# Banded attention beside a gated MLP on one NeuronCore: 64-key blocks, and two head groups on the two partition halves

## The chip, the cores and the metric

The kernel runs on one core of a Trainium2 chip. Its metric is the device time of one execution, in microseconds (us). Three runs of the kernel before took 259.98, 260.29 and 259.19 us; their median is 259.98 us. The core has five engines that run side by side and wait for each other through semaphores: TensorE (PE: matmuls, each preceded by a weight load, PEld), VectorE (DVE), ScalarE (ACT), GpSimd (POOL) and SyncE (SP, which here issues DMAs). Matmul results go to PSUM, which has eight banks of 512 float32 columns on each of 128 partitions.

## The reference

```python
xn = layernorm(x)                                   # x: 2048 tokens x 512
# A: attention, 32 heads of 16, a band of 256 keys back from each query
q, k, v = split(xn @ wqkv)
scores  = q @ k.T * 16 ** -0.5
mask    = (i - j >= 0) & (i - j < 256)
o       = softmax(where(mask, scores, -1e9)) @ v
# B: gated MLP with a 2048 x 2048 mix over tokens
z       = gelu(xn @ w_in); z1, z2 = z[..., :688], layernorm(z[..., 688:])
g       = w_sp @ z2 + b_sp[:, None]
out     = x + o @ wo + (z1 * g) @ w_out             # bfloat16 in and out
```

## The kernel before

The first stage (to about 84 us of the span) normalizes and transposes x, computes z (`zp`, L280), and most of the 48 units of q, k and v (`pj_`, L111 and L129). q is stored twice with the odd or the even heads zeroed (`qpad`), so that a strip of 32 partitions holds two heads, e = 0 and 1, and a *group* G of 8 heads fills 128 partitions as four strips s. v is stored with a column of ones behind each head, so that P times V also gives the softmax's sums.

The second stage is written out by hand: the string `ORDER` is a list of steps, and the program issues them in that order on every engine.

- `S` takes the next block of scores (`do_scores`). For a pair of query tiles J (256 queries) and a group G there are two kinds, "P" and "Q": four strips of a 32-row by 128-column tile of the array (128 keys, the columns are queries of two heads), 8 matmuls of 256 columns. A third kind, "D", serves two groups at once: the corners of the band, in 32 x 64 tiles, 32 matmuls of 128 columns. Each `S` fills two tiles of the PSUM pool `ps_s` (three tiles of two banks), and ACT takes the exponential of each tile into `E` or `ED` (L608, L583).
- `m` multiplies the result by a 0/1 mask on DVE (L611).
- `p` is P times V of one (J, G) (`pv`, L519): 56 matmuls in 128 x 32 tiles, four at a time, for the four strips. Their output `o` is one bank of the pool `ps_x` (two banks). DVE transposes it (L526). For the corners a copy `vh` of v with one half of the partitions zeroed is loaded by DMA (`load_half`).
- `n` divides by the sums and transposes again (`normalize`, L532 to L542) into `oT`.
- `q`, `g`, `f` begin a unit of the last four v tiles, of the token mix (`gf`, L433, 16 matmuls of 344 columns) or of the output (`fo`, L469 and L476, 10 matmuls of 512 columns: six with `uT`, four with `oT`); a number goes on with the unit for so many matmuls. These use the whole 128 x 128 array and the pool `ps_x`. After the last `g` of a tile, u is transposed by a DMA into `uT`, and `f` adds x and stores.

So PE's order is fixed: runs of whole-array matmuls, with `S` and `p` set between them. `check_sums` looks at all softmax sums at the end (after output tile 13); a branch recomputes attention with the maximum subtracted if a sum is out of range.

Of the kernel before, what the change touches and what calls it, by code (L numbers as in the profile page):

```python
# [8 lines left out]
P = 128  # L9
# [5 lines left out]
S_TOK = 2048  # L15
# [3 lines left out]
VW = DH + 1  # L19
VROW = H * VW + DH  # L20
F = 1376
# [13 lines left out]
PAD = 64  # L35
NM = NB + 1
# [4 lines left out]

ORDER = """
S q4 q4 S q4 q4 S g m 8 S m 8 g3 S 7 S m 6 p S p S g n m 8 S m 8 g3 S n 7 S m 6 g2 S 11 S 3
g m 6 S m 10 S p p S g n m 11 S n 5 g5 S m 11 S p p S f n m 7 S 3 g m 5 S n 11 S p p S g n m
10 S m 6 f3 S m 7 S p p S g n n 10 S m 6 g4 S m n 12 f1 S m 6 S 3 g5 S m 11 S p p S f n m 7
S 3 g m 5 S n 11 S p p S g n m 10 S 6 g m 4 S m 12 S p p S f n n 6 S 4 f m 3 S m 7 g1 S m 9
S n 6 g4 S m 12 S p p S f n m 6 S 4 g m 5 S n 11 S p p S f n m 7 S 3 g m 5 S m 11 S p p S g
n n 16 S f m m 6 S 4 g n 4 S m 12 S p p S g n m 9 S m 7 f2 S n 7 S 1 f m 10 S p p S g n m 16
g1 S m n 8 S 7 g m 16 S p p S g n n 16 g1 S m 15 f1 S m 6 S 3 g5 S m 11 S p p S g n m 16 f1
S m 9 S p g n m 16 g n 16 p f n 10 f10 f10 f10  # L50
"""

@with_exitstack
def kernel(
# [22 lines left out]
    kT = pers.tile([P, NG, PAD + S_TOK], BF, name="kT")  # L77
    v_y = pers.tile([P, NM, VROW], BF, name="v_y")
# [4 lines left out]
    maskY = pers.tile([P, P], BF, name="maskY")  # L83
    maskD = pers.tile([P, P], BF, name="maskD")
    maskC = pers.tile([P, PAD], BF, name="maskC")
# [5 lines left out]
    xnT = pq.tile([P, NC, PAD + S_TOK], BF, name="xnT")  # L91
    wqkv = pq.tile([P, NC, 3 * D], BF, name="wqkv")
    r_all = pers.tile([P, NJ * NG, 16], F32, name="r_all")
# [10 lines left out]
    def qkv_unit(b, i, k):  # L104
        t0 = PAD + b * 512
# [20 lines left out]
        else:  # L126
# [7 lines left out]
            parts = [(0, PAD, NB), (PAD, P, 0)] if m == 0 else [(0, P, m)]  # L134
            for p0, p1, mo in parts:
                nc.vector.tensor_copy(
                    out=v_y[p0:p1, mo, 0 : H * VW].rearrange("p (h w) -> p h w", w=VW)[:, :, 0:DH],
                    in_=pt[p0:p1, :].rearrange("p (h d) -> p h d", d=DH),
                )

    qkv_list = [(b, i) for b in range(4) for i in range(12) if (b, i) != (0, 8)] + [(0, 8)]

    with ExitStack() as actx:
# [54 lines left out]
        def setup_late():  # L198
            nc.vector.memset(kT[:, :, 0:PAD], 0.0)
# [5 lines left out]
            nc.vector.memset(v_y[0:PAD, 0, :], 0.0)  # L205
            nc.vector.memset(v_y[PAD:P, NB, :], 0.0)
            nc.vector.tensor_tensor(
                out=maskC[:], in0=maskD[:, 0:PAD], in1=maskD[:, PAD:P], op=ALU.add
            )

        for m, off in ((maskY, 0), (maskD, -PAD)):
            nc.gpsimd.memset(m[:], 1.0)
            nc.gpsimd.affine_select(
                out=m[:, 0:PAD], in_=m[:, 0:PAD], pattern=[[-1, PAD]],
                compare_op=ALU.is_gt, fill=0.0, base=off, channel_multiplier=1,
            )
            nc.gpsimd.affine_select(
                out=m[:, PAD:P], in_=m[:, PAD:P], pattern=[[1, PAD]],
                compare_op=ALU.is_ge, fill=0.0, base=PAD + off, channel_multiplier=-1,
# [42 lines left out]
        def transposes(n, xn):  # L262
            if n >= 8:
                nc.sync.dma_start_transpose(
                    out=xnT[:, :, PAD + n * P : PAD + (n + 1) * P], in_=xn[:]
# [7 lines left out]
            nc.scalar.copy(out=xnT[:, :, PAD + n * P : PAD + (n + 1) * P], in_=tp[:])  # L273

        def z_half(n, half):
            zp = ps_s.tile([P, 2, 512], F32, name="zp", tag="S")
            for c in range(NC):
                for j in range(2):
# [3 lines left out]
                        lhsT=xnT[:, c, PAD + n * P : PAD + (n + 1) * P],  # L282
# [43 lines left out]
        for n in range(NB):  # L326
# [7 lines left out]
            if n == NB - 3:  # L334
                nc.vector.tensor_copy(out=xnT[:, :, 0:PAD], in_=xnT[:, :, S_TOK : PAD + S_TOK])
# [46 lines left out]
    ep = ctx.enter_context(tc.tile_pool(name="ep", bufs=4))  # L382
    cp = ctx.enter_context(tc.tile_pool(name="cp", bufs=2))

    late_ctx = ctx.enter_context(ExitStack())
    late_pool = []
    v_half = []

    def late():
        if not late_pool:  # L390
# [5 lines left out]
            for i in range(2):  # L396
                vh = late_pool[0].tile([P, 4, VROW], BF, name=f"vh{i}")
                nc.gpsimd.memset(vh[PAD:P, 0:2, :], 0.0)
                nc.gpsimd.memset(vh[0:PAD, 2:4, :], 0.0)
                v_half.append(vh)  # L400
        return late_pool[0]

    def load_half(J):
        late()
        vh = v_half[J % 2]
        nc.sync.dma_start(out=vh[0:PAD, 0:2, :], in_=v_y[0:PAD, 2 * J + 1 : 2 * J + 3, :])
        if J > 0:
            nc.sync.dma_start(out=vh[PAD:P, 2:4, :], in_=v_y[PAD:P, 2 * J - 2 : 2 * J, :])
# [53 lines left out]
    def f_work(t, c0):  # L462
# [11 lines left out]
        q0 = (1 - t % 2) * P  # L474
# [15 lines left out]
    ED = {}  # L490
# [3 lines left out]
    def pv(J, G):  # L494
        Et = E[(J, G)]
        Ed = ED[(J, G // 2)]
        g = G % 2
        o = ps_x.tile([P, 512], F32, name="o", tag="f")
        for e in range(2):
            c0 = e * 256  # L500
            vh = v_half[J % 2]
# [50 lines left out]
    def do_scores(J, G, kind):  # L552
# [12 lines left out]
        if kind == "D":  # L565
            ED[(J, G // 2)] = late().tile([P, 32, PAD], BF, name="ED", bufs=2)
            if G == 0 and J == 0:
                load_half(0)
# [295 lines left out]
```

## Time and profile before

| | |
|---|---|
| median of 3 runs | 259.98 us (259.19 to 260.29) |
| profiled execution | 259.87 us, span 258.2 us |
| PE busy | 252.7 us, 98% of the span, 3877 matmuls |
| ACT busy | 196.5 us, 76% |
| DVE busy | 205.1 us, 79% |
| second stage: first `S` to last output add | 84.1 to 255.1 us |
| ACT in 100 to 200 us of the span | 18.96 to 19.75 us busy in each 20 us |
| chain that ended last | PE 96% |
| granted TensorE clock | 1.00 |

A busy PE here means that some matmul was in flight. Matmuls overlap, so the time that a block of them takes is read from the start of its first to the start of what follows it.

### The profile page before, as it was taken

The numbers are of one execution on the slowest core, as the hardware profiler recorded it, in microseconds if no ns is written. First come the engines' busy times: TensorE is split into PE (matmuls) and PEld (weight loads), VectorE is DVE, ScalarE is ACT, GpSimd is POOL, SyncE is SP. The second block draws the span as 40 slices with busy tenths as digits, with TensorE's granted clock in tenths as the row PEclk, the third lists the DMA queues.
The fourth block names the chain that finished last, engine by engine and source line by source line (L and its number), as shares of the span: only waits on it lengthen the run. The fifth ranks groups of instructions, "written<-read, shape, count | busy, mean of one in ns | idle before, by whom it ended". The sixth has DMA issues, their size and how long they took to land.

```text
span 258.2 us, 8833 instructions
## 1 busy us (share of the span) xinstructions
PE 252.7 (98%) x3877; PEld 142.4 (55%) x3877; DVE 205.1 (79%) x425; ACT 196.5 (76%) x236; POOL 20.2 (8%) x49
## 2 busy tenths in 40 slices
PE   8999999999999999999999999999999999999994
PEld 2665555555555455655654655555564655646553
DVE  4895997875657889598889689898889978858784
ACT  2777547456456899999999999999998988689600
POOL 4120312111011240000000000000000000000000
PEclk9999999999999999999999999999999999999999
DMA  7994021027400207575244709654637644654332
GB/s 218 369 252 143 0 43 41 0 45 124 79 0 4 62 6 156 112 158 94 68 66 135 173 28 159 106 138 82 98 43 177 84 116 90 120 111 108 74 55 67
DMA packets 64683, 25.85 MB, mean 100 GB/s; under 512 B 53649, under 2 KB 63169, under 8 KB 64641
## 3 DMA queue, kind: packets, MB, share of 16 engines
q1 hardware_dynamic: 63152, 24.22, 44.4%
q10 hardware_dynamic: 1488, 1.03, 1.3%
q8 instruction: 31, 0.51, 0.8%
q14 instruction: 12, 0.09, 0.1%
HBM read 8.41 MB, written 2.10 MB: 41 GB/s over the span
## 4 chain that ended last, share of the span: by engine, by line
PE 96%; DVE 1%; DMA 1%; issue 0%; POOL 0%
PE gf L433 31%; PE zp L280 15%; PE S L558 11%; PE o L519 9%; PE fo L469 9%; PE pj_o L111 7%; PE fo L476 6%; PE pj_f L111 4%; PE pj_f L129 3%; PE pj_o L129 2%; DMA xt<-in_A_x_dram 1%; PE tp L270 1%; DVE stats L228 1%; POOL rs L238 0%; DVE xo L481 0%
## 5 line engine op out<-in xcount | busy, mean ns | idle before, releaser
L608 ACT ACTIVATE E<-S 128x1024 bf16<-128x1024 f32 (+1 forms) x128 | 117.6, 1007 | 8.7 <-PE S L558 8.5
L433 PE MATMUL gf<-z2n,wspT 128*128 128x344 bf16 x512 | 83.3, 310 | 0.0
L433 PEld LDWEIGHTS <-wspT 128*128 128x128 bf16 x512 | 46.7, 98 | 28.6 <-issue 5.5
L280 PE MATMUL zp<-w_in_sb,xnT 128*128 128x344 bf16 x256 | 41.7, 309 | 0.0
L611 DVE TENSOR_TENSOR E<-E,maskY 128x2048 bf16<-128x2048 bf16 (+2 forms) x36 | 37.9, 1058 | 2.5 <-ACT E L608 2.4
L280 PEld LDWEIGHTS <-xnT 128*128 128x128 bf16 x256 | 24.8, 98 | 15.3 <-ACT xnT L273 0.2
L558 PE MATMUL S<-qpad,kT 32*64 32x128 bf16 (+1 forms) x1008 | 32.9, 246 | 0.1
L583 ACT ACTIVATE ED<-S 128x1024 bf16<-128x1024 f32 x32 | 31.0, 1023 | 2.3 <-PE S L558 2.3
L526 DVE STREAM_TRANSPOSE ot<-o 128x512 f32<-128x512 f32 x32 | 22.3, 715 | 8.4 <-PE o L519 8.3
L558 PEld LDWEIGHTS <-kT 32*64 32x64 bf16 (+1 forms) x1008 | 12.3, 98 | 22.7 <-issue 21.6
L469 PE MATMUL fo<-w_out_sb,uT 128*128 128x512 bf16 (+1 forms) x102 | 24.6, 368 | 0.0
L439 DVE SCALAR_TENSOR_TENSOR u<-gf,b_all,z 128x344 bf16<-128x344 f32 x32 | 18.2, 567 | 7.3 <-PE gf L433 6.4
L519 PE MATMUL o<-E,v_y 128*32 128x128 bf16 (+1 forms) x736 | 23.3, 239 | 0.3 <-issue 0.3
L519 PE MATMUL o<-ED,vh 128*32 128x64 bf16 x960 | 21.2, 193 | 0.0
L111 PE MATMUL pj_o<-xnT,wqkv 128*128 128x512 bf16 x80 | 20.5, 379 | 0.0
L287 ACT ACTIVATE z<-zp 128x688 bf16<-128x688 f32 x16 | 11.9, 743 | 11.1 <-PE zp L280 11.1
L287 ACT ACTIVATE z2n<-zp 128x688 bf16<-128x688 f32 x16 | 11.9, 743 | 10.3 <-PE zp L280 10.3
L111 PEld LDWEIGHTS <-wqkv 128*128 128x128 bf16 x128 | 12.5, 98 | 12.6
L122 DVE TENSOR_SCALAR qpad<-qt,hmask 128x512 bf16<-128x512 bf16 x32 | 9.7, 346 | 12.2 <-ACT qt L120 12.2
L611 DVE TENSOR_TENSOR ED<-ED,maskC 128x2048 bf16<-128x2048 bf16 x16 | 19.4, 1210 | 0.0
L476 PE MATMUL fo<-wo_sb,oT 128*128 128x512 bf16 (+1 forms) x68 | 17.7, 368 | 0.0
L519 PEld LDWEIGHTS <-v_y 128*32 128x32 bf16 x736 | 15.2, 97 | 4.0 <-issue 3.6
(68 smaller groups left out, 234.8 us busy)
## 6 DMA issues: line engine op xcount, KB each, us to landing
vh<-v_y SPq DMA_DIRECT2D x15, 140.0 KB, 3.5
xo<-in_A_x_dram SPq DMA_DIRECT2D x16, 128.0 KB, 3.4
out_dram<-xo SPq DMA_DIRECT2D x15, 128.0 KB, 2.0
xt<-in_A_x_dram SPq DMA_DIRECT2D x3, 512.0 KB, 9.8
wqkv<-in_A_wqkv_dram SPq DMA_DIRECT2D x1, 1536.0 KB, 10.2
w_in_sb<-in_B_w_in_dram ACTq DMA_DIRECT2D x2, 344.0 KB, 5.8
w_in_sb<-in_B_w_in_dram SPq DMA_DIRECT2D x2, 344.0 KB, 5.4
w_out_sb<-in_B_w_out_dram SPq DMA_DIRECT2D x1, 640.0 KB, 6.1
```

The lines of the kernel that those rows point to most:

```text
L111: nc.tensor.matmul(pt[:], lhsT=wqkv[:, c, w0 : w0 + P], rhs=xnT[:, c, t0 : t0 + 512], start=(c == 0), stop=(c == NC - 1),)
L280: nc.tensor.matmul(zp[:, j, 0:HALF], lhsT=xnT[:, c, PAD + n * P : PAD + (n + 1) * P], rhs=w_in_sb[:, c, f0 : f0 + HALF], start=(c == 0), s ...
L287: nc.scalar.activation(out=dst.rearrange("p (j f) -> p j f", j=2), in_=zp[:, :, 0:HALF], func=ACT.Gelu_apprx_tanh,)
L433: nc.tensor.matmul(gf[:, 0:HALF], lhsT=wspT[t][:, c, :], rhs=z2n[:, c, j * HALF : (j + 1) * HALF], start=(c == 0), stop=(c == NB - 1),)
L469: nc.tensor.matmul(fo[:, 0:w], lhsT=uTs[t][:, ch, :], rhs=w_out_sb[:, ch, c0 : c0 + w], start=(ch == 0), stop=False,)
L476: nc.tensor.matmul(fo[:, 0:w], lhsT=oTs[t // 2][:, c, q0 : q0 + P], rhs=wo_sb[:, c, c0 : c0 + w], start=False, stop=(c == NC - 1),)
L519: nc.tensor.matmul(o[32 * s : 32 * s + 32, c0 + r0 : c0 + r0 + n], lhsT=v[:, m, h * VW : h * VW + 32], rhs=rhs(s), start=(i == 0), stop=(i ...
L526: nc.vector.transpose(out=ot[:].rearrange("p b j -> p (b j)"), in_=o[:])
L558: nc.tensor.matmul(out, lhsT=kT[32 * s : 32 * s + 32, g, k0 : k0 + nk], rhs=qpad[J // 2][32 * s : 32 * s + 32, g, :, qs - q00 : qs - q00 + ...
L583: nc.scalar.activation(out=Ed[:, 16 * i : 16 * i + 16, :], in_=S[i][:].rearrange("p b (x q) -> p (b x) q", q=PAD), func=ACT.Exp, scale=SM_ ...
L608: nc.scalar.activation(out=o, in_=w, func=ACT.Exp, scale=SM_SCALE)
L611: nc.vector.tensor_tensor(out=out, in0=in0, in1=mask.unsqueeze(1).to_broadcast([P, in0.shape[1], in0.shape[2]]), op=ALU.mult,)
```

## The change

Keys are cut into blocks of 64 where they were cut into tiles of 128. A pair of query tiles then sees eight key blocks, and each block serves a run of 64-query pieces (one to four). The table `BURSTS` lists these as (block, first piece, pieces, column), packed into five `S` steps of 256 columns each (three for J = 0), with no separate corner kind. All scores use 32 x 64 tiles: two head groups at once, one on each half of the output partitions. So `E` holds 64 keys of one group on partitions 0 to 63 and 64 keys of the other on 64 to 127. P times V contracts over 64 rows and handles both groups at once in 64 x 32 tiles, eight at a time: 128 matmuls for each J and pair of groups (64 for J = 0), with an output of two banks that now comes from `ps_s`, the pool of the scores. Where a group's v lies on the other half of the partitions, it is loaded across by DMA (`load_cross`) in place of `load_half`. The masks shrink to 1024, 2048 and 1024 columns for each J and pair of groups. `E` has one buffer for each pair of groups where it had four in all. The 64-token shift of the keys (`PAD`) goes, and `ORDER` is a new list: 76 `S` (80 before), 16 `p` (32), 48 `m` (48), the same `q`, `g` and `f`.

```diff
-PAD = 64
+KB = 64
+EW = 5 * 256
+BURSTS_FIRST = [
+    [(4, 0, 4, 0)],
+    [(7, 3, 1, 256), (5, 1, 3, 320)],
+    [(6, 2, 2, 512)],
+]
+BURSTS = [
+    [(3, 0, 4, 0)],
+    [(4, 0, 4, 256)],
+    [(2, 0, 3, 512), (7, 3, 1, 704)],
+    [(0, 0, 1, 768), (5, 1, 3, 832)],
+    [(1, 0, 2, 1024), (6, 2, 2, 1152)],
+]
+MASKS_FIRST = [(0, 64), (256, 128), (512, 64)]
+MASKS = [(192, 128), (640, 256), (1088, 128)]
 ORDER = """
-S q4 q4 S q4 q4 S g m 8 S m 8 g3 S 7 S m 6 p S p S g n m 8 S m 8 g3 S n 7 S m 6 g2 S 11 S 3
...
-S m 9 S p g n m 16 g n 16 p f n 10 f10 f10 f10
+S q4 q4 S q4 m q3 S 1 g6 S 10 S g3 m 2 m 4 m S 5 m 1 p m S 1 g9 p n S 7 g1 S 3 n 4 m 4 S 4 f1 m
+3 S 6 S g9 m p S 7 g1 S 1 m 10 S 4 g6 S 9 m 1 S g6 m 3 S 6 n 1 f1 p S 6 S 3 n g7 S 9 S f7 S 3 g3
+m 1 m S 11 S 1 f1 m 5 S m 4 g1 p S 5 m 3 S 3 m 4 g5 S 4 m 4 S 3 g5 p S 4 n 5 S 2 g9 S 1 n 6 f2 S
+6 S 1 m 1 g2 m 1 m 3 S 6 m 2 p S 1 m 1 g6 S 4 n 4 p S 2 g8 S 8 g1 S m 7 m 2 m S 6 f3 S 1 n 6 S
+f2 m 3 p S 3 m 2 g1 S 2 m 10 S 3 g9 S p 6 S 1 f5 S 5 g4 n S 4 n 5 S 3 g9 S 4 m 3 f1 S 7 m 1 S 1
+g3 m 4 S 8 p S 1 g4 m 4 S m 8 g2 S 4 m 6 S 4 f4 p S 6 S g5 n 5 S 4 m 2 g1 m 3 S 10 n 1 S m 1 g9
+m S 7 f1 m p S 4 m 3 S 2 f3 p S 3 m 4 S g9 S 1 m 6 g4 S 6 m 2 n 1 p S 3 g7 S 2 n 3 m 4 g1 n 1 S
+7 m 2 S 5 f8 m 2 f1 p 7 n 2 f10 f10 f10
 """
...
+    def load_cross(J):
+        vx = cp.tile([P, 2, VXROW], BF, name="vx", bufs=3)
+        v_cross[J] = vx
+        nc.gpsimd.memset(vx[:, :, 3 * VG :], 0.0)
+        for h in range(2):
+            own, other = slice(h * KB, h * KB + KB), slice(KB - h * KB, P - h * KB)
+            nc.sync.dma_start(
+                out=vx[own, :, 0 : 3 * VG],
+                in_=v_y[other, 2 * J : 2 * J + 2, h * VG : (h + 3) * VG],
+            )
...
+    def pv(J, g):
+        Et = E.pop((J, g))
+        o = ps_s.tile([P, 2, 512], F32, name="S", tag="S")
+        terms = sorted((t for burst in bursts(J) for t in burst), key=lambda t: -t[2])
+        n = len(terms)
+        terms = [terms[i // 2 if i % 2 == 0 else n - 1 - i // 2] for i in range(n)]
         for e in range(2):
+            for i, (k, i0, ni, c0) in enumerate(terms):
+                m = 4 * J - 4 + k
                 for s in range(4):
+                    for h in range(2):
+                        part = slice(h * KB, h * KB + KB)
...
+                        q0 = e * 256 + i0 * KB
+                        nc.tensor.matmul(
+                            o[32 * s : 32 * s + 32, h, q0 : q0 + ni * KB],
+                            lhsT=v, rhs=Et[part, s, e, c0 : c0 + ni * KB],
+                            start=(i == 0), stop=(i == n - 1),
+                        )
+        ot = late().tile([P, 2, 16, 32], F32, name="ot", bufs=2)
+        turned[(J, g)] = ot
+        nc.vector.transpose(
+            out=ot[:].rearrange("p h b j -> p (h b j)"), in_=o[:].rearrange("p h c -> p (h c)")
+        )
...
+    def do_scores(J, g, burst):
+        if burst == 0:
+            pool = late() if (2 * J + g) % 2 else ep
+            E[(J, g)] = pool.tile([P, 4, 2, EW], BF, name=f"E{g}")
+            if g == 1 and J + 1 < NJ:
+                load_cross(J + 1)
+        S = [ps_s.tile([P, 2, 512], F32, name="S", tag="S") for _ in range(2)]
+        terms = bursts(J)[burst]
+        b0 = min(t[3] for t in terms)
+        for k, i0, ni, c0 in terms:
+            k0 = (4 * J - 4 + k) * KB
+            q0 = J % 2 * 256 + i0 * KB
+            for s in range(4):
+                for h in range(2):
+                    o = S[s // 2][h * KB : h * KB + KB, s % 2, :]
+                    nc.tensor.matmul(
+                        o.rearrange("p (e q) -> p e q", e=2)[:, :, c0 - b0 : c0 - b0 + ni * KB],
+                        lhsT=kT[32 * s : 32 * s + 32, 2 * g + h, k0 : k0 + KB],
+                        rhs=qpad[J // 2][32 * s : 32 * s + 32, 2 * g + h, :, q0 : q0 + ni * KB],
+                        start=True, stop=True,
+                    )
+        w = sum(t[2] for t in terms) * KB
+        Et = E[(J, g)]
+        for i in range(2):
+            nc.scalar.activation(
+                out=Et[:, 2 * i : 2 * i + 2, :, b0 : b0 + w].rearrange("p s e q -> p (s e) q"),
+                in_=S[i][:].rearrange("p s (e q) -> p (s e) q", e=2)[:, :, 0:w],
+                func=ACT.Exp, scale=SM_SCALE,
+            )
```

`normalize` does for two groups at once what it did for one (one reciprocal of 32 sums, two multiplications, one transpose of 512 columns), and `do_mask` multiplies the three column ranges of `MASKS` with one mask tile for both halves.

More of the change, by code (lines that the diff above doesn't have):

```diff
@@ L529, in normalize, with bursts @@
[L529 to L540 removed]
+    def bursts(J):
+        return BURSTS if J else BURSTS_FIRST
@@ L793 @@
     rows = []
-    masks = [x for x in groups if x[2] != "P"]
-    units = [(J, G) for J in range(NJ) for G in range(NG)]
+    masks = [(J, g, i) for J, g in pairs for i in range(3)]
+    units = list(pairs)
+    load_cross(0)
     work = {
```

280 lines of the change are left out of this document (87 added, 193 removed).

## The prediction

> **What bounds the kernel now.** First the page's busy table, its slices and its chain:
>
> ```profile
> PE 252.7 (98%) x3877; PEld 142.4 (55%) x3877; DVE 205.1 (79%) x425; ACT 196.5 (76%) x236; POOL 20.2 (8%) x49
> ...
> ACT  2777547456456899999999999999998988689600
> ...
> PE 96%; DVE 1%; DMA 1%; issue 0%; POOL 0%
> ```
>
> PE sets the end, and in the stage of `ORDER` (84 to 255 us) ACT is full as well. So a gain must come out of PE's time, and ACT must not become later. Next, ACT's groups with their shapes kept apart:
>
> ```profile
> L608 ACT ACTIVATE E<-S 128x1024 bf16<-128x1024 f32 x120 | 113.7, 1033 | 8.7 <-PE S L558 8.5
> L583 ACT ACTIVATE ED<-S 128x1024 bf16<-128x1024 f32 x32 | 31.0, 1023 | 2.3 <-PE S L558 2.3
> L608 ACT ACTIVATE E<-S 128x512 bf16<-128x512 f32 x8 | 4.4, 623 | 0.0
> ```
>
> An exponential of 1024 columns costs 113.7 / 120 = 0.95 us, a step `S` 1.9 us. Third, PE's timeline around one `p p`, to see what a block of small tiles costs (start, length, ..., the lengths overlap, so differences of starts count):
>
> ```profile
> 132.02 0.40 PE L558 MATMUL S<-qpad,kT 32*128 32x256 bf16 x8
> 132.34 0.35 PE L519 MATMUL o<-E,v_y 128*32 128x256 bf16 x8
> 132.52 0.23 PE L519 MATMUL o<-ED,vh 128*32 128x64 bf16 x8
> 132.58 0.23 PE L519 MATMUL o<-E,v_y 128*32 128x128 bf16 x4
> 132.63 0.23 PE L519 MATMUL o<-ED,vh 128*32 128x64 bf16 x8
> 132.69 0.34 PE L519 MATMUL o<-E,v_y 128*32 128x256 bf16 x8
> 132.86 0.23 PE L519 MATMUL o<-ED,vh 128*32 128x64 bf16 x8
> ...
> 133.81 0.43 PE L558 MATMUL S<-qpad,kT 32*64 32x128 bf16 x32
> 134.17 1.63 PE L433 MATMUL gf<-z2n,wspT 128*128 128x344 bf16 x10
> 135.73 0.52 PE L558 MATMUL S<-qpad,kT 32*128 32x256 bf16 x8
> ```
>
> Four tiles at once: two rounds of 64 columns take 0.057, a round of 128 takes 0.057, 256 and 128 together 0.166, so 256 alone 0.11. The D block (32 matmuls, eight tiles at once) takes 0.36. Ten `gf` of 0.146 take 1.56, so leaving a run of whole-array matmuls costs 0.10; every change of tile shape does. The trace's starts within a round lie 3.3 ns apart, weight loads between them.
>
> Last, a place where PE stands still in the middle of a `p`:
>
> ```profile
> 125.11 0.22 PE L519 MATMUL o<-E,v_y 128*32 128x128 bf16 x1
> 125.65 0.24 PE L519 MATMUL o<-E,v_y 128*32 128x128 bf16 x3 [0.32 <-issue]
> ```
>
> No buffer or operand ends this wait. Against a round of 0.057 it costs 0.49. The page's DMA table explains it:
>
> ```profile
> q8 instruction: 31, 0.51, 0.8%
> ```
>
> These 31 packets and 0.51 MB for PE's 2 x 3877 instructions are PE's code, some 250 instructions (125 matmuls) each. Two of three such stops lie at PE's records 2496 and 4288, 7 x 256 apart, the third at 3008: boundaries of 256 instructions. In the DMA records a packet starts 0 to 3.1 us after PE passes a boundary (once 1.0 before), takes 1.0 to 1.4, and at those three stops PE went on 1.4 to 1.5 after the packet's end. So the next 256 instructions must not be used up sooner than 3 to 4 us. In the rest of the stage they last 3.5 to 10 us, but for one span.
>
> **The change, part by part,** against the profiled execution's own 259.87 us (span 258.2 and 1.7 around it; the median is 259.98).
>
> *P times V.* The two G of a J took 1.46 (chain rows of x112) in 13 cases, 2 x 0.79 in the last, for J = 0 2 x 0.56 and 1.0: 19.0 + 1.6 + 2.1 = 22.7. After, a step has for each e rounds of 256, 64, 256, 64, 192, 128, 192 and 128 columns: 2 x (0.110 + 0.028 + 0.083 + 0.057) = 0.56, twice 1.11, with the shape change and the first loads 1.23; for J = 0 half the rounds, 0.67. 14 x 1.23 + 2 x 0.67 = 18.5: **-4.2**. It supposes that 64 x 32 tiles run eight at once, which no row shows; the nearest are D (eight at once, 32 x 64) and this `p` (four at once). Bounds: -4.2, and +12.5 (each round doubled). I take -4.2: D has both row strips and column halves.
>
> *Scores.* A single round of 512 columns in eight tiles costs what two rounds of 256 in four tiles do, 0.33; steps of two rounds 0.34 to 0.36. Five sum to 1.70, before 4 x 0.33 + 0.36 = 1.68: +0.02 x 14. J = 0 has three steps (0.91) for five (1.46), twice: -1.1. Sum **-0.85**.
>
> *The new order.* It cuts the whole-array work into 77 runs where there were 66: 11 x 0.10 = **+1.1**.
>
> *Waits for PSUM.* `p` now takes a tile of the pool of three. The next `S` then needs both exponentials of the one before it, and the second `S` after `p` the DVE transposition of o. Counted off `ORDER`, two `S` with a `p` between stand 2.5 to 3.1 us apart; needed are 0.12 + 0.30 (from the first matmul of an S to the last, from there to ACT) + 0.90 + 1.02 (two exponentials back to back) + 0.09 (to PE) = 2.4. The second `S` comes 1.6 us or more after `p`; needed are 0.3 + about 1.25 (512 columns take 0.72). So both waits are just covered, nothing taken; if DVE is in a mask of 1.2 us then, up to 0.5 each, 8 in all. Two waits of `S` for ACT before (J = 0, at 96.1 and 110.0, the blocks 0.61 and 0.57 long for 0.36 and 0.33) have no counterpart: **-0.45**.
>
> *ACT* sheds 4 full and 4 half exponentials, 6 us of 149; 143 us fit into 84 to 240 us, `S` standing 2.05 apart on average for 1.9 of ACT. *DVE* loses a third of its mask columns (-19 us), joins two transpositions into one: hidden, PE is later. *DMA*: eight crossings of two DMAs for 15 of `vh`, on SP's queue in the same places, a J ahead, with tiny memsets on POOL in front of `u`'s, a tile ahead: nothing; if late, `p` waits up to the 3.5 us of a landing, once a J. `E`'s single buffer per pair is freed by a `p` that `ORDER` puts ahead of the next pair's first `S`: nothing.
>
> *The tail.* After the last `p`, DVE's chain to the output is longer: transposition 1.25 for 0.72, two multiplications, one transposition of 512: +1.25, then the add, `check_sums` (1.8) and the next add free PSUM for the last `fo`. It waited 0.1 to 0.2 before, now about 1.1: **+0.9**.
>
> Sum so far -3.5: 256.4.
>
> *Code.* Some 4053 matmuls for 3877, and a full `p` is 256 instructions, one whole packet, run in 1.23 us. Where a boundary falls shortly ahead of a `p`, the next 256 are gone in the `p` and an `S`. Laying the costs above along `ORDER` (two instructions a matmul), 12 of 26 boundaries of the stage have the next one 2.3 to 3.1 us later. Before, only three spans were as short: 3.16 and 3.03 (stops of 0.13 and 0.32) and 2.76, whose packet came early (no stop). From PE's passing to usable code, the 25 packets of that stage needed 1.5 to 5.7 us, mostly 2.9 to 3.9. Bounds for the 12: nothing, and (3.7 - 2.7) x 12 = 12, or 16 where transfers collide with packets. I take 0.55 each, **+6.6**, more than the two stops of like spans because the spans are shorter, less than the middle of all packets because a boundary ahead of a `p` is read early while PE still has whole-array work. The stops of before (0.49 + 0.32 + 0.13) go: **-0.9**. Sum -3.5 + 6.6 - 0.9 = +2.2: **262.1 us**.
>
> [...]
>
> **The rivals.**
> 1. *The code comes in time: faster.* If PE's sequencer stands 64 instructions ahead, as the packet that came 1.0 early suggests, it passes a boundary 1.5 us before PE does and the spans suffice. Stops under 3.5 in all: 255.5 to 259.0, most likely 256.5. [...] For it: 22 of 25 boundaries cost nothing. Against: the spans there were longer. It decides when a packet is usable 2.6 us after the boundary.
> 2. *Packets behind DMA transposes.* At 120.98 and 164.84 the packet came 2.3 and 3.1 us after PE, amid `wspT` transfers. At 0.85 to 1.2 us for each of the 12, 10 to 14 in all: 265.5 to 269.5, say 267.
> 3. *The row halves of P times V do not overlap.* A `p` costs 2.34, 1.23 twice: +12.5 on P times V in place of -4.2, so 255.5 + 16.7 = 272, with the code stops gone, since such a `p` gives a packet time. For it: no row has this tile. Against: D. [...]
>
> **How the numbers follow.** The forecast 0.50 (stops of 3.5 to 10: 259 to 265.5), rival 1 0.30, rival 2 0.13, rival 3 0.07. A measurement tells some 0.5% (1.3 us) from no change: faster is below 258.7, slower above 261.3. Rival 1 gives 0.28 faster and 0.02 same; of the forecast a third is within: 0.17; the rest, 0.53, is slower. The range from 255.5 to 268.5 leaves out rival 3 and the edges.
>
> **What would show it.** Right: waits "issue" on PE, on matmuls or loads inside or just after L524's `o`, some ten of 0.2 to 1.5 us, 128 matmuls apart or a multiple; an undisturbed `p` of 1.23; `S` of 0.33 to 0.36. Rival 1: no such waits, span near 255. Rival 2: waits over 1 us beside a full DMA slice. Rival 3: rounds of 256 columns 0.22 apart. The prediction is wrong in another way if PE waits for ACT at the `S` after a `p`, or for DVE at the one after that.

## The result, and the profile after

The changed kernel takes **270.81 us** (median of 4 runs, 269.12 to 273.33), the kernel before beside it 260.13: ratio **1.039, 95% interval 1.033 to 1.046** (the run of 273.33, 1.6% above the fastest, counts as slow and is left out of the ratio). The prediction was 262.1 in a range of 255.5 to 268.5, with a chance of 0.53 for slower. The sign is right, the time is outside the range. The profiled execution of after took 271.59 us with a span of 269.8: 11.6 more than the span of before. All accounts below are made on these two spans.

From the page of after, the busy table, PE's slices, the chain that ended last and the code packets:

```profile
PE 249.7 (93%) x4029; PEld 137.7 (51%) x4053; DVE 178.6 (66%) x367; ACT 192.0 (71%) x228; POOL 16.6 (6%) x52
...
PE   6999999999998999798999898999999989799980
...
q8 instruction: 32, 0.52, 0.9%
...
PE 86%; issue 4%; DVE 3%; DMA 2%; ACT 2%; SPq 1%; POOL 0%; DVEq 0%
```

PE was busy 98% of a shorter span before and 93% now, and "issue" stands in the chain with 4%, where it had 0. So the longer time is PE standing still, not PE working more. (24 of the 4053 matmul records are missing in this trace, all of matmuls of 512 columns; each leaves 0.22 without a start, and six waits of `fo` for "issue" in the trace, of 0.2 each, are no more than that.) L576 is the scores `S`, L442 is `gf`, L478 is `fo`. L524 is `p`: the view calls its output S as well, since it takes a tile of that pool. What PE waited for, in the view of waits (us in total, times, longest):

```profile
PE S L524 <- issue: 2.4, 2, 1.6
PE S L576 <- issue: 2.2, 3, 1.4
...
PE S L576 <- DVE r_all L539: 1.2, 1, 1.2
...
PE S L576 <- ACT E L585: 1.1, 2, 0.7
PE gf L442 <- issue: 1.1, 1, 1.1
...
PE fo L478 <- DVE xo L490: 0.9, 1, 0.9
```

"Issue" stops lie inside `p`, inside `S` and inside `gf`: no one kind of work, and no buffer. Two of them in PE's timeline (start, length, ..., the idle time before in brackets):

```profile
111.04 0.40 PE L576 MATMUL S<-qpad,kT 32*64 32x384 bf16 x9
112.86 0.26 PE L576 MATMUL S<-qpad,kT 32*64 32x128 bf16 x7 [1.42 <-issue]
...
235.37 0.24 PE L524 MATMUL S<-E,v_y 64*32 64x192 bf16 x1 [1.59 <-issue]
```

An `S` stops after 9 of its 16 matmuls. Counting PE's weight loads from the start, eight stops lie where 96 + 128 k pairs of load and matmul have gone, that is 256 instructions or a multiple apart (a q8 packet has 16384 bytes), at 112.86, 126.00, 151.47, 164.71, 168.44, 218.14, 235.37 and 246.97, and each ends 1.31 to 1.60 us after the end of a q8 packet. Taken between starts, less the usual distance, they cost 1.58, 0.80, 1.28, 0.56, 0.97, 1.26, 1.75 and 0.35 us: 8.55, where before had 0.94. The one at 218.14 is the row "DVE r_all" above, and the one at 164.71 is part of "ACT E": the view names the last operand that came, the records the packet that ended 1.31 and 1.34 before.

The rest came at the end. Records of the final branch in the two traces, which no view of busy time shows (start in us, length in ns; the rest of each line is put together from the records after it):

```
before  256.12   352  PE  COMPARE_BRANCH   next instruction: PE 0.41 us, DVE 0.60 us after its branch; span ends 2.04 after
after   264.69  4082  PE  COMPARE_BRANCH   next instruction: PE 4.14 us, DVE 3.43 us after its branch; span ends 5.12 after
```

A code packet of PE starts at 265.71 and ends at 267.48, while PE stands in that branch.

### The profile page after: what moved, and what is told of

Its sections match the earlier page's. It is cut to its first block, busy times and chain, and to the rows that moved or that the text cites. A ratio compares the mean times of both kernels' runs of the same rounds, so it can differ in the third digit from the quotient of the medians.

```text
span 269.8 us, 9076 instructions
## 1 busy us (share of the span) xinstructions
PE 249.7 (93%) x4029; PEld 137.7 (51%) x4053; DVE 178.6 (66%) x367; ACT 192.0 (71%) x228; POOL 16.6 (6%) x52
## 4 chain that ended last, share of the span: by engine, by line
PE 86%; issue 4%; DVE 3%; DMA 2%; ACT 2%; SPq 1%; POOL 0%; DVEq 0%
PE gf L442 29%; PE zp L291 14%; PE S L576 10%; PE S L524 8%; PE fo L478 6%; PE pj_o L128 5%; PE fo L485 5%; PE pj_f L128 4%; PE pj_o L146 3%; PE pj_f L146 2%; ACT E L585 1%; DMA xt<-in_A_x_dram 1%; DVE xo L490 1%; DMA vx<-v_y 1%; SPq L463 1%
## 5 line engine op out<-in xcount | busy, mean ns | idle before, releaser
L585 ACT ACTIVATE E<-S 128x1024 bf16<-128x1024 f32 x152 | 142.6, 1015 | 24.5 <-PE S L576 23.5
L442 PE MATMUL gf<-z2n,wspT 128*128 128x344 bf16 x512 | 85.7, 310 | 1.1 <-issue 1.1
L442 PEld LDWEIGHTS <-wspT 128*128 128x128 bf16 x512 | 45.7, 98 | 32.7 <-issue 12.3
L291 PE MATMUL zp<-w_in_sb,xnT 128*128 128x344 bf16 x256 | 41.9, 309 | 0.0
L604 DVE TENSOR_TENSOR E<-E,maskFD 128x1024 bf16<-128x1024 bf16 (+2 forms) x48 | 38.2, 812 | 5.1 <-ACT E L585 4.9
L576 PE MATMUL S<-qpad,kT 32*64 32x512 bf16 (+3 forms) x960 | 33.4, 310 | 4.7 <-issue 2.2
L531 DVE STREAM_TRANSPOSE ot<-S 128x1024 f32<-128x1024 f32 x16 | 20.0, 1250 | 22.8 <-PE S L524 22.8
L576 PEld LDWEIGHTS <-kT 32*64 32x64 bf16 x960 | 11.4, 102 | 27.0 <-issue 25.7
L478 PE MATMUL fo<-w_out_sb,uT 128*128 128x512 bf16 (+1 forms) x87 | 23.1, 365 | 2.3 <-issue 1.0
L524 PE MATMUL S<-E,v_y 64*32 64x256 bf16 (+2 forms) x960 | 21.9, 231 | 1.6 <-issue 1.6
L524 PE MATMUL S<-E,vx 64*32 64x256 bf16 (+2 forms) x960 | 21.9, 232 | 0.8 <-issue 0.8
L524 PEld LDWEIGHTS <-vx 64*32 64x32 bf16 x960 | 18.1, 90 | 6.5 <-issue 6.4
L490 DVE TENSOR_TENSOR xo<-fo,xo 128x512 bf16<-128x512 f32 (+1 forms) x17 | 11.1, 656 | 13.4 <-PE fo L485 13.3
L524 PEld LDWEIGHTS <-v_y 64*32 64x32 bf16 x960 | 18.9, 90 | 1.5 <-issue 1.5
L139 DVE TENSOR_SCALAR qpad<-qt,hmask 128x512 bf16<-128x512 bf16 x32 | 9.7, 345 | 11.3 <-ACT qt L137 11.3
```

The lines of the kernel that those rows point to most:

```text
L291: nc.tensor.matmul(zp[:, j, 0:HALF], lhsT=xnT[:, c, n * P : (n + 1) * P], rhs=w_in_sb[:, c, f0 : f0 + HALF], start=(c == 0), stop=(c == NC ...
L442: nc.tensor.matmul(gf[:, 0:HALF], lhsT=wspT[t][:, c, :], rhs=z2n[:, c, j * HALF : (j + 1) * HALF], start=(c == 0), stop=(c == NB - 1),)
L478: nc.tensor.matmul(fo[:, 0:w], lhsT=uTs[t][:, ch, :], rhs=w_out_sb[:, ch, c0 : c0 + w], start=(ch == 0), stop=False,)
L524: nc.tensor.matmul(o[32 * s : 32 * s + 32, h, q0 : q0 + ni * KB], lhsT=v, rhs=Et[part, s, e, c0 : c0 + ni * KB], start=(i == 0), stop=(i = ...
L531: nc.vector.transpose(out=ot[:].rearrange("p h b j -> p (h b j)"), in_=o[:].rearrange("p h c -> p (h c)"))
L576: nc.tensor.matmul(o.rearrange("p (e q) -> p e q", e=2)[:, :, c0 - b0 : c0 - b0 + ni * KB], lhsT=kT[32 * s : 32 * s + 32, 2 * g + h, k0 : ...
```

## Two theories

*Code:* PE, and at the branch DVE too, wait for their next instructions; what counts is where the boundaries of 256 instructions fall in the work, and where the target of the final jump (over the body of the branch, which these inputs don't run) lies. *Tiles:* the time lies in the small tiles, the shape changes and PSUM, and the stops are only where it shows. They are told apart by moving the boundaries and leaving the work as it is.

## Experiments on the code

**The same work half a packet further on.** Added to after:

```diff
-WARM = 11
+WARM = 4
+SHIFT = 71
...
+        for _ in range(SHIFT):
+            nc.tensor.matmul(heat[:, 0:8], lhsT=idle[:, 0:P], rhs=idle[:, 0:8], start=True, stop=True)
```

> Kernel after, with seven of the eleven idle matmuls at the start made small and 64 small ones added, so that the same work stands 64 matmuls (128 instructions, half a code packet) further on in PE's code. Code theory: a p of 128 matmuls then always has a boundary near its middle and never a whole packet inside it. Laying the measured instruction times (its stops taken out) under the shifted boundaries, with 3.6 us from passing a boundary to usable code, no span of the stage is shorter than 3.6: the 8.55 us of stops go to about 0.1. At the end the jump's target on PE (290 instructions behind the branch) would lie in the next packet instead of the one after that, so PE no longer waits, but DVE, which waited until 268.15 against PE's 268.83, still does: -0.6. Span 260.7, time about 262.4, against 271.6. Tile theory (the added time lies in the smaller tiles, the added shape changes and PSUM waits): idle matmuls at the start change nothing, 271 within 1.

Measured: **264.47 us** (264.01 to 264.69), ratio 1.0155 (1.0125 to 1.0185), span 263.0. All waits of PE in its view:

```profile
PE tp L284 <- DVE xn L270: 1.3, 2, 1.0
PE heat L202 <- DVE warm L207: 1.3, 1, 1.3
PE fo L481 <- DVE xo L493: 0.9, 1, 0.9
PE S L579 <- ACT E L588: 0.7, 1, 0.7
PE S L527 <- issue: 0.3, 1, 0.3
```

The stops are gone but for 0.4 and 0.2, the wait for "DVE r_all" is gone with them, and the stage from the first `S` to PE's end takes 170.5 us where it took 179.1 (before: 170.5). Sixty-four more idle matmuls, and seven of the old ones made small, made the kernel 6.3 us faster with the same tiles behind them; the tile theory falls as the account of the 8.55 us. That the gain was not 9 has its own reason: the first `S` starts 1.84 later (85.83 for 83.99), because `zp` starts 0.24 later and its first 24 matmuls took 5.39 us behind small idle matmuls where they took 3.79 behind full ones. PE's branch took 358 ns, but DVE went on only 3.98 after its own, and the span still ended 5.02 after the branch, as expected.

**A smaller shift**, the same edit with nine full and 18 small idle matmuls:

> Kernel after with 16 small idle matmuls added at the start (32 instructions). Code theory: the same reckoning gives the stops 16.5 us where it gives 9.0 for the kernel as it is, because more spans hold a whole p and its neighbours: +7.5, less 0.6 at the final branch, so about 278.5. Tile theory: 271 within 1.

Measured: 270.53 us (269.35 to 272.33). A miss: the time is what the tile theory forecast. But the trace shows that the stops did move, to other places (112.48, 125.64, 150.68, 164.46, 191.28, 216.87, 230.30, 235.95), but they cost 7.6 us, not 16.5, so the time alone could not tell the theories apart. The reckoning took 3.6 us from passing a boundary to usable code everywhere. In after's own trace 13 spans had less than 3.6 us of work, and only the eight whose packet started 0.9 to 2.1 us after PE passed the boundary before cost anything; for the other five it had started between 0.9 ahead and 0.3 behind. In this run more boundaries are of the second kind. The second half of the reckoning holds at every stop of both runs: PE goes on 1.3 to 1.7 us after the packet's end.

**The branch alone:** the last loop of the If's body taken out of after (44 lines that these inputs don't run; nothing ahead of the branch changes).

```diff
-        with tc.For_i(0, NB, 1) as t:
-            row0 = t * P
...
-            nc.sync.dma_start(out=out2[bass.ds(row0, P), :], in_=xo[:])
```

> Kernel after without the last loop in the body of the If (the fallback's output loop, not run on these inputs), 119 instructions of PE fewer behind the branch; everything before the branch is the same. Code theory: the jump's target comes within the packet after the branch's, PE's COMPARE_BRANCH takes 0.35 us instead of 4.08, and if DVE's target comes near too, the end is 3.7 us earlier: about 267.9. The eight stops stay where they are (8.5). Rival: the 4 us of the branch are the flag's transfer or a semaphore of the end, and stay: 271.6.

Measured: **268.63 us** (268.10 to 270.51), ratio 1.031 (1.028 to 1.035). PE's branch took 373 ns, DVE went on after 0.58, and the span ended 1.87 after the branch instead of 5.12. Code behind the branch that never runs cost 3.2 us at the end. The medians lie 2.2 apart, and the spans of the profiled executions only 1.3, since the stage took 1.8 longer in this one than in that of after. The stops in the stage stayed: 8.5 us in seven, six of them at the same loads as in after.

**The kernel before, shifted** by 32 matmuls (eight full and 35 small idle ones):

> Kernel before with 32 small idle matmuls added at the start (64 instructions). Code theory: the reckoning gives its stops 9.9 us in place of 2.9 (measured 0.94), so some +6; and the target of the jump at its end moves from the packet after the branch's to the one after that, +3.7. In all +6 to +10: 266 to 270. If only the new kernel's tiles matter, 260 within 1.

Measured: **268.67 us** (266.01 to 269.67), ratio 1.029 (1.022 to 1.036): the old kernel becomes as slow as the new one. Three of its stops in PE's timeline:

```profile
150.22 0.21 PE L522 MATMUL o<-ED,vh 128*32 128x64 bf16 x3 [0.95 <-issue]
...
166.93 0.36 PE L561 MATMUL S<-qpad,kT 32*64 32x128 bf16 x21 [0.87 <-issue]
...
243.41 0.25 PE L561 MATMUL S<-qpad,kT 32*64 32x128 bf16 x5 [1.32 <-issue]
```

The code stops in the stage sum to some 5.6, the stage starts 1.7 later, and PE's branch takes 3333 ns where it took 352. One more stop, of 0.7 at 228.85, lies at no boundary: the view puts it down to a load of `w_sp`. So 0.94 of stops in before was where its boundaries happened to lie, and so were the 8.55 of after.

**The transfers beside the code.** In the records of after, the packets ahead of the stops at 112.86, 164.71, 218.14 and 235.37 started 1.3 to 2.1 us after PE passed their boundary, and in that time the 16 DMA engines were fully busy with the transposing loads of `w_sp` (mean share 0.98 and above in these four stretches); ahead of the other four they started after 0.9 to 1.4, with the engines idle (share 0.04 to 0.10). That points at rival 2 of the prediction. The kernel after, without these loads from t = 2 on (its token mix then uses the first two tiles again and again, so that its output is not the reference's):

```diff
             if t + 2 < NB:
-                load_wsp(t + 2)
+                wspT[t + 2] = wspT[t]
```

> Kernel after with the transposing loads of w_sp left out from t = 2 on (the token mix uses the first two tiles of w_sp again and again, so its values are not the reference's): the same instructions on PE in the same code blocks, but 14 transfers of 3 to 5 us less on the DMA engines. In after, the packets ahead of four of the eight stops (those at 112.86, 164.71, 218.14 and 235.37) started 1.3 to 2.1 us after PE passed the boundary, with the 16 DMA engines fully busy in that time, and those ahead of the other four 0.9 to 1.4 after it, with the engines idle. If packets of code wait behind these transfers (rival 2 of the prediction), each of the first four becomes some 0.6 shorter, about 2.5 us in all, and the stops sum to about 6: 268.5. If the transfers are beside the point, they stay at 8.5 and the time at 271 within 1.

Measured: **266.59 us** (265.93 to 267.06), ratio 1.024 (1.019 to 1.029), 4.2 less than after and more than expected. PE's waits for code in its view, to be set against 2.4, 2.2 and 1.1 with longest of 1.6, 1.4 and 1.1 in after:

```profile
PE S L576 <- issue: 1.2, 4, 0.4
PE S L524 <- issue: 1.1, 3, 0.7
...
PE gf L442 <- issue: 0.4, 1, 0.4
```

Eight stops are left, none over 0.88, together 3.9 us for 8.55, and the stage from the first `S` to PE's end takes 174.1 for 179.1. No packet of the stage starts later than 1.6 after PE passes its boundary, most after 0.7 to 1.3; in after some took 2.0 to 2.7. So the boundaries say where PE can stop, and with the transfers went 4.6 of the 8.55 us. The four stops behind busy DMA engines fell from 5.2 to 1.3; the other four fell from 3.4 to 2.3, and for that 1.1 no cause is shown (one new stop of 0.3 came). The shift above takes away nearly all without touching a transfer, since then no span is short (none under 3.6 us by the reckoning).

**The shift without its side effects.** In place of idle matmuls, 16 projection units have their four matmuls of 512 columns cut into eight of 256 (64 pairs more), and 72 small memsets move DVE's code:

```diff
+    split = [True] * 16
...
+        n = 2 if split and split.pop() else 1
+        cols = [slice(h * 512 // n, (h + 1) * 512 // n) for h in range(n)]
...
+        for _ in range(36):
+            nc.vector.memset(blank[:], 0.0)
...
+            if n in (6, 8, 10):
+                for _ in range(12):
+                    nc.vector.memset(blank[:], 0.0)
```

> Kernel after with the same half-packet shift of PE's code, but got by cutting 64 projection matmuls of 512 columns into two of 256 (a 256 takes 0.109, a 512 0.2157: +0.15 in all) instead of small idle matmuls at the start, which had delayed the stage of ORDER by 1.8 us; and 72 one-column memsets added on DVE in its idle time, which put DVE's final jump in the same code block as its target. Code theory: no stop over 0.3 in the stage (-8.3 against after), no engine waits at the final branch (-3.0): span 269.8 - 8.3 - 3.0 + 0.15 = 258.6, time about 260.3, so that after without its code stops is even with before, and not the 256.4 of the prediction's sum without code. Rival: the end after the branch stays at 5 us (DVE waits for something else than code): 263.4.

Measured: 265.09 us (264.75 to 265.48), span 262.9. The end is as expected: branch 353 ns, DVE on after 0.60, span end 2.04 behind. But the 36 memsets at the start were not hidden: "PE tp" waited 2.8 for DVE and `zp` ran slowly behind that gap (43.4 us busy for 41.9 in after), so that the first `S` came at 88.17. The miss is that of the edit. `a_even` below puts the memsets elsewhere.

## Experiments on the other terms

**The tail.** On top of `a_split64`, `check_sums` in two parts:

```diff
+        if t == NB - 4:
+            check_sums(0, 14)
         if t == NB - 3:
-            check_sums()
+            check_sums(14, 16)
```

> a_split64 with the check of the sums in two: the sums of J = 0 to 6 after the add of t = 12, the last 64 columns of r_all alone after the add of t = 13. If the last fo waits for PSUM because DVE checks 512 columns (0.41 + 0.69 + 0.69) between two adds, it waits no longer (0.93 to 1.10 in after): span 0.9 below a_split64, time about 259.4. Rival: the chain transposition, multiplications, transposition is what is late; then 0.3 at most.

Measured: 264.55 us (263.21 to 265.27), 0.54 less in the median. The ranges of the two overlap, and in the profiled executions the first `S` came 0.86 later and two code stops (waits of 0.5 and 0.3) were gone, so the timeline decides and not the median. The last two units of `fo` in a_pads64, with the check whole:

```profile
253.71 0.60 PE L488 MATMUL fo<-wo_sb,oT 128*128 128x256 bf16 x4
255.25 0.81 PE L481 MATMUL fo<-w_out_sb,uT 128*128 128x256 bf16 x6 [0.93 <-DVE xo L493]
```

and the last two of a_early, with the check in two, from the end of the unit before them:

```profile
255.72 0.60 PE L496 MATMUL fo<-wo_sb,oT 128*128 128x512 bf16 x2 [0.17 <-DVE oT L567]
256.29 0.81 PE L489 MATMUL fo<-w_out_sb,uT 128*128 128x256 bf16 x6
256.94 0.60 PE L496 MATMUL fo<-wo_sb,oT 128*128 128x256 bf16 x4
257.50 0.81 PE L489 MATMUL fo<-w_out_sb,uT 128*128 128x256 bf16 x6
```

The wait of 0.93 for PSUM ahead of the last unit is gone; DVE's chain to `oT` now shows two units earlier. Between starts, the gaps of the tail went from 1.09 to 0.33 + 0.13 + 0.12: half the wait was the check, half is the chain behind it.

**The memsets in their place**: on top of `a_early`, eight in each of nine blocks of the projection stage:

```diff
-        for _ in range(36):
-            nc.vector.memset(blank[:], 0.0)
...
-            if n in (6, 8, 10):
-                for _ in range(12):
+            if 5 <= n < 14:
+                for _ in range(8):
```

> a_early with the 72 memsets moved from DVE's first 4 us (where 36 of them made the first transposes of xn 2.3 to 3.2 us late and PE's start slow) to eight in each of nine blocks of the projection stage. The stage of ORDER takes what it took in a_early (first S to PE's last matmul 169.6 against 179.1 in after and 170.5 in before), and starts at 84.2 again: PE ends at 253.8, span 257.7, time 259.4 against 260 of before: even within 0.5 %. If the late start was not the memsets' doing, it stays near 264.

Measured: **260.13 us** (259.64 to 260.71), ratio **1.002** (1.0006 to 1.0034), span 258.3 with the first `S` at 84.06. Without code stops (one of 0.72 is left) and with the lighter tail the new work is as fast as the old. The prediction's sum without code, 256.4, does not come back.

**P times V.** Two kernels on top of a_split64, each run once and read by its timeline; both leave part of P times V out, so that their output is not the reference's. The first has half the columns (DVE then turns the same columns twice):

```diff
-                        q0 = e * 256 + i0 * KB
+                        q0 = e * 128 + i0 * KB // 2
+                        nw = ni * KB // 2
...
-                            o[32 * s : 32 * s + 32, h, q0 : q0 + ni * KB],
-                            lhsT=v, rhs=Et[part, s, e, c0 : c0 + ni * KB],
+                            o[32 * s : 32 * s + 32, h, q0 : q0 + nw],
+                            lhsT=v, rhs=Et[part, s, e, c0 : c0 + nw],
```

> a_split64 with every matmul of P times V at half its columns (32, 64, 96 and 128; the other half of the queries is left out, and DVE turns the same columns twice in four pieces): as many instructions, half the streaming. Issue theory (a load and its matmul in a 64 x 32 tile can't follow the last pair sooner than 8.2 to 9 ns once the first 28 or so are out): a full p still takes about 1.0 to 1.1 us with its shape change, against 1.325. Streaming theory of the prediction: 0.56 + 0.12 = 0.68.

The second has the same number of columns in fewer matmuls, over key blocks that are not those of the reference:

```diff
+        if J:
+            terms = [(3 + i % 2, 0, 4, 256 * i) for i in range(5)]
```

> a_split64 with the eight rounds of each e of a full p (256, 64, 256, 64, 192, 128, 192, 128) replaced by five of 256 columns: the same 1280 columns in 80 matmuls instead of 128; the blocks of keys are not those of the reference, so P times V itself is left out and only its shape kept. Issue theory: every round is now longer than its issue, so p takes 10 x 0.108 + 0.12 = 1.2 us instead of 1.325. If p is longer for another reason (tiles that share something, so that a column costs more), it stays at 1.3. Code boundaries move with every p, so stops may come back elsewhere; the p without a stop counts.

The first and last rows of a full `p`, and the `S` behind it, in PE's timeline of a_even (128 matmuls, all columns):

```profile
136.54 0.28 PE L535 MATMUL S<-E,vx 64*32 64x256 bf16 x1
...
137.72 0.22 PE L535 MATMUL S<-E,v_y 64*32 64x128 bf16 x1
137.87 0.42 PE L587 MATMUL S<-qpad,kT 32*64 32x512 bf16 x8
```

of a_half_p (128 matmuls, half the columns):

```profile
124.28 0.23 PE L536 MATMUL S<-E,vx 64*32 64x128 bf16 x1
...
125.32 0.20 PE L536 MATMUL S<-E,v_y 64*32 64x64 bf16 x1
125.45 0.37 PE L591 MATMUL S<-qpad,kT 32*64 32x384 bf16 x8
```

and of a_wide_p (80 matmuls, all columns):

```profile
124.38 0.28 PE L537 MATMUL S<-E,vx 64*32 64x256 bf16 x1
...
125.40 0.27 PE L537 MATMUL S<-E,v_y 64*32 64x256 bf16 x1
125.60 0.41 PE L589 MATMUL S<-qpad,kT 32*64 32x384 bf16 x12
```

From the first matmul to the next block: 1.33, **1.173** and **1.216** us. Half the streaming saves 0.15 where 0.55 would be its share; three eighths of the matmuls fewer save 0.11 with every column kept. In a_half_p the first four rounds, 32 pairs, start 3 to 4 ns apart within a round; from the fifth on the rounds of eight pairs start 66 to 67 ns apart, whatever their width: 8.3 ns a pair. In a_wide_p they start 109 apart, the streaming time of 256 columns. So the eight 64 x 32 tiles do run at once, and a `p` of 128 matmuls is bound by how fast pairs of load and matmul come.

**The order of the rounds**, on top of a_even. First the two long starts, then from short to long:

```diff
-            for i, (k, i0, ni, c0) in enumerate(terms):
+        wide = [t for t in terms if t[2] == 4]
+        rest = sorted(terms, key=lambda t: t[2])
+        rest.remove(wide[0])
+        rounds = [(e, t) for t in [wide[0]] + rest for e in range(2)]
+        for i, (e, (k, i0, ni, c0)) in enumerate(rounds):
```

> a_even with the sixteen rounds of a full p in another order: the first 256 of both e, then the rounds of 64, 128, 192 and the other 256. Issue theory: some 28 pairs of load and matmul stand ready at 3.3 ns when p begins, and rounds of 256 (0.107 for eight pairs) let more come in than they use; short rounds just behind two long ones then run at their streaming time, and p comes near its streaming sum, 1.11 + 0.12 = 1.23 instead of 1.325: -0.09 x 14 = -1.3, time 258.1. If a pair costs 8.3 ns wherever it stands and nothing is kept ready, no change.

Measured: 261.80 us, ratio 1.008 (1.006 to 1.010), a `p` 1.454: slower, the opposite of what was expected. Then from long to short:

```diff
+        rounds = [(e, t) for t in sorted(terms, key=lambda t: -t[2]) for e in range(2)]
```

> a_even with the rounds of p from long to short, both e together: four of 256, four of 192, four of 128, four of 64. What a_half_p and a_order show is that some 32 pairs of load and matmul are ready when p begins and pair i of the others becomes available about 0.35 + (i - 32) x 0.0083 us after it, whatever stands before. Long rounds first then run at their streaming time (0.107, 0.080) while pairs gather, and the short ones find theirs ready: the last pair, available at 1.14, is the bound, p 1.20 to 1.24 instead of 1.325, -0.1 x 14: span 1.2 to 1.6 below a_even's 258.3. If pairs don't gather behind long rounds (as the slow p of a_order could also mean), a p is 4 x (0.107 + 0.080 + 0.067 + 0.067) + 0.1 = 1.38, +0.8.

Measured: 261.22 us, ratio 1.005 (1.003 to 1.007), a `p` 1.417: again slower, near the second value. The starts of its rounds, four of each width, in ns from the first:

```
a_long  p: 0 120 229 338 | 447 530 613 695 | 778 833 889 965 | 1032 1098 1165 1232
a_even  p: 0 120 149 259 308 390 456 531 596 698 751 839 897 967 1041 1119
```

Behind eight long rounds only two short ones run at their streaming time (55 for 128 columns), then each takes 67 again. It is as if only some 16 pairs gathered ahead (an estimate from these rows) and were used up in two rounds. Long and short in turn, as the change has them, is the best of the three; that it is so because it draws on that small store at every second round is argued, not shown.

**The first exponential.** Not named in the prediction: the change also puts a v unit back to its place in the list of projection units. On top of a_even:

```diff
-    qkv_list = [(b, i) for b in range(4) for i in range(12)]
+    qkv_list = [(b, i) for b in range(4) for i in range(12) if (b, i) != (1, 8)] + [(1, 8)]
```

> a_even with one line of the list of projection units as in before, in kind: a v unit, (1, 8), is taken out of its place and done last. In before (0, 8) was done last, so the unit just ahead of the stage was a k unit finished on ACT at 83.87; in after the stage is reached one unit later in the list, ACT's copy of that kT starts at 84.17, the load of the exponential's table at 84.77 instead of 83.90, and the first exponential at 86.2 instead of 85.3. If that is why the second S waits 0.92 at 87.2, the wait goes to 0.1: span 0.8 below a_even's 258.3. If the wait is that of the new S for its three PSUM tiles at any pace, it stays.

ACT's timeline around the start of the stage, of before,

```profile
83.29 0.58 ACT L117 CAST kT<-pj_o 128x512 bf16<-128x512 f32 x1 [0.23 <-PE pj_o L111]
83.90 1.28 ACT L372 ACT_TABLE_LOAD   x1
...
85.30 2.89 ACT L608 ACTIVATE E<-S 128x1024 bf16<-128x1024 f32 x4
```

of after, and PE's timeline there,

```profile
84.10 0.59 ACT L134 CAST kT<-pj_f 128x512 bf16<-128x512 f32 x1 [0.23 <-PE pj_f L128]
84.70 1.28 ACT L381 ACT_TABLE_LOAD   x1
...
86.11 2.83 ACT L585 ACTIVATE E<-S 128x1024 bf16<-128x1024 f32 x3
```

```profile
87.17 0.41 PE L576 MATMUL S<-qpad,kT 32*64 32x128 bf16 x12 [0.74 <-ACT E L585]
```

and of a_list the same two:

```profile
84.00 1.28 ACT L389 ACT_TABLE_LOAD   x1
...
85.41 4.72 ACT L596 ACTIVATE E<-S 128x1024 bf16<-128x1024 f32 x6
```

```profile
86.34 0.54 PE L587 MATMUL S<-qpad,kT 32*64 32x128 bf16 x16
```

Measured: **259.47 us** (258.74 to 260.60), ratio **0.9986** (0.9970 to 1.0002), span 257.1, and the second `S` runs through without a gap. One unit's place in a list of 48 was worth 0.7 us in the median (1.2 in the spans, of which 0.5 is a smaller code stop).

**All together**, with one projection unit more cut in two:

> a_even with the rounds of a_long, the list of a_list, and 17 instead of 16 projection units cut in two (four pairs more of shift, against the one stop left, 0.7 at 142.6). By the first theory of each: -1.3 - 0.8 - 0.6, span 255.6, time 257.4, that is 0.990 of before. If long rounds first don't help and the wait stays: 258 to 259 of span, even with before.

Measured: 260.11 us, ratio 1.001 (0.9996 to 1.0027). The list gives what it gave (1.1 less than a_long) and the last stop is gone, but the long rounds first (a `p` 1.416) take it back. The best version run is a_list, which is even with before within the interval: none of them beats it for certain.

## Why the prediction was wrong

By its own steps, against the spans of before and after (the whole-array runs, the scores and their waits measured in a_pads64, which has no missing records; stops of code taken out of every other row):

| step | predicted | measured |
|---|---|---|
| code stops in the stage, less those of before | +5.7 | +7.6 |
| final branch | not named | +3.1 |
| P times V | -4.2 | -2.2 |
| scores | -0.85 | +0.4 |
| new order, 11 more runs | +1.1 | +1.1 |
| waits of `S` for PSUM | -0.45 | +0.35 |
| tail | +0.9 | +0.95 |
| sum | +2.2 | +11.3 of 11.6 |

- **Code** was the right mechanism, named with its boundaries, and 1.9 too small. The prediction had 12 short spans at 0.55; there were 13, of which eight cost 1.07 on average and five nothing. Of the 8.55, 4.6 are those of rival 2, packets behind transfers, as far as the loads taken away in a_quiet show it; the prediction had kept rival 2 apart with 0.13 as another case, when both act at once. The trace of before already had that case: its largest stop, the 0.49 that the prediction shows, had 4.4 us of work ahead of it since the last boundary, and its packet started more than 2 us after PE passed that boundary, with the DMA engines full (share 1.01 from 121.0 to 123.3). The larger failure is that the step ended with the stage: the same shortage at the final jump cost 3.1 and stands in no line of the prediction. Ahead of the branch stand 8106 loads and matmuls, 234 past the last boundary; the target lies some 290 PE instructions further, so that by this count it fell into the packet after the next; with 119 instructions fewer behind the branch (a_short_if) the branch took 0.37 us where it had taken 4.08.
- **P times V:** the estimate took the gap of 3.3 ns between matmuls of one round as the price of a pair. That holds for the first 32 pairs of a `p`; then a pair takes 8.3 ns (a_half_p), and a round of 64 columns takes as long as one of some 160 (67 ns, at 109 ns for 256 columns). A full `p` is 1.325 for the 1.23 predicted, and some are 1.40 to 1.44. Rival 3, no overlap of the row halves, is excluded: a round of 256 takes 0.109 in 64 x 32 tiles too.
- **Scores:** one round of 512 columns takes 0.354, not 0.33, and a step of two rounds 0.357. Five steps sum to 1.78 for the 1.70 of the prediction, the three of J = 0 to 0.96 for 0.91: 0.08 x 14 + 0.05 x 2 = 1.2, which eats the gain of J = 0 and more.
- **Waits of `S`:** the two waits of before did go. The new one at 87.17 (a step of 1.33 in place of 0.36) was not a matter of the three PSUM tiles but of one kT copy on ACT (0.59 us) ahead of the load of the exponential's table (1.28): in a_list that load starts at 84.00 for 84.70, and the second `S` has no wait.
- **New order and tail** came out as predicted, and apart from these two waits, at 87.17 and in the tail, ACT, DVE and the crossing of v by DMA were hidden as predicted: the view of waits of a_pads64 has no other row for them in the stage.
- **Rival 1** is excluded: the packets don't come in time. Its 64 instructions ahead agree with the 32 pairs that start 3 to 4 ns apart at the head of a `p` (a_half_p), but the packets ahead of the eight stops of after started 0.9 to 2.1 us after PE passed the boundary.

With the two code terms alone set right the forecast is 262.1 + 1.9 + 3.1 = 267.1, still inside the range; the three other errors, 2.0 + 1.25 + 0.8 = 4.05 and all to the same side, did the rest.

## What to carry to other kernels

- These long unrolled programs had their stops where their code boundaries fell, not where their work is hard: after had 8.55 us of them, and 0.6 with the same work half a packet further on. Where small instructions come in bursts of a boundary's length, count the instructions ahead of them: half a packet of shift was worth 6 us here, and 64 instructions made the old kernel 8.5 us slower (1.7 of it by the later start that the edit brought, 0.7 by a load of `w_sp`). Transfers at the wrong moment made such stops longer: four fell from 5.2 to 1.3 us without the loads of `w_sp`. Compare two versions of such a kernel only after trying both at another shift.
- Code that a branch jumps over had a price, 3.2 us at the end of this kernel: PE's branch took 4.08 us with the target in the block of 256 instructions after the next, and 0.36 and 0.37 with it in the next one (a_pads64, a_short_if). Keep it there, and look at the other engines too: with 72 more instructions ahead of the branch DVE went on 0.60 us after its branch, where it had taken 3.43 (a_split64).
- Cost small matmuls by pairs of load and matmul, not by columns: here 8.3 ns each, once the first 32 are out, wherever a round of eight streams for less than 67 ns.

## What was not expected of the hardware

- With the target too far, the final jump held PE 3.3 to 4.3 us and DVE 3.2 to 4.0 (the upper value of PE and the lower of DVE in a_quiet); with the target near, PE's branch takes 0.35 to 0.45 and DVE goes on after 0.60. Each engine has its own, and mending PE alone (a_pads64) moved the end, counted from the branch, by only 0.1.
- Small idle matmuls (8 columns) or a wait of 2 to 3 us ahead of the first projections made those slow: the stage of `ORDER` began 1.6 to 1.8 us late with the first, and 4.2 late with a first wait of 2.3. In a_pads64 the first 12 `zp` start some 0.287 apart, and then 0.146, which is their distance in after from the start. It was not taken apart further.
- In four of the 14 full `p` of a_half_p one round comes 0.08 to 0.13 late, 0.6 to 1.0 us after the start; in a_even some do, and in a_wide_p none. Its cause stays open, as does why some packets start up to 0.9 us ahead of PE's passing.
